# RWKV-7 recurrence and GELU MLP on one core: b' and k' of chunks 4 to 11 turned by VectorE from a second load, and another order of the first chunks

## The chip, the cores and the metric

The kernel runs on one core of a Trainium2 chip. The time of a kernel is the device time of one execution in microseconds (us), given as the median of several runs. TensorE is PE in the profile (PEld is its weight load), VectorE is DVE, ScalarE is ACT, GpSimd is POOL, and SyncE is SP; SPq is SyncE's queue, from which nearly all transfers (DMAs) are issued in order.

## The reference

For each of 4 x 8 pairs of batch and head, a 40 x 40 state is carried over 768 steps; the outputs, joined over the heads to 3072 rows of 320, go through an MLP.

```
for t in range(S):
    y[t]  = r[t] @ state
    Sa    = state @ a[t]
    state = state * w[t] - outer(Sa, b[t]) + outer(v[t], k[t])
x   = y, (B, H, S, D) -> (B*S, H*D)
out = gelu_exact(x @ w_in) @ w_out          # 320 -> 2048 -> 320
```

All inputs but the two MLP weights are float32. The weights come as 64-bit floats, which the kernel turns into float32 itself.

## The kernel before

**Chunks.** The 768 steps are cut into 12 chunks of 64 (c = 0 to 11). Inside a chunk the recurrence is written with matrices over the 64 steps. With cumulative decays (`sums`: a product of the logs of w with a triangle, then Exp), b and k are divided by the decay so far (`scale_b`, `scale_k`: `nb` and `ks`, with time on the partitions) and a is multiplied by it (`scale_a`). `make_N` and `make_A` multiply a' with b' and k' over the head dimension; for these products b' and k' must lie with the head dimension on the partitions, that is turned. N's triangular inverse is made on GpSimd, in 31 columns of two instructions each (`start_inverse`, L604 and L606): the 32 x 32 blocks go out to DRAM and come back spread over all partitions (tiles N, Nb), and the result returns the same way (`store_inverse`, `fetch_inverse`: tiles W, inv, Tt). The corner blocks are joined by small products (`corner`, `joined`: J). From these come X, sa, M, and QY, which holds the new state and the outputs (`make_X` to `make_QY`, `outputs`), and a second load of v and r makes RV.

**Turning.** `flip` (L411) turns a tile on TensorE, as eight 128 x 128 products with the identity into PSUM; ACT copies the result to SBUF. b' (`turn_b`, tile nT), k' (`turn_k`, tile kT) and the state (`turn_state`) are turned so in every chunk. a, r and v are turned so in chunks 0 to 2 only (NT = 3). From chunk 3 on `fetch_pairs` (L147) loads them in a layout of pairs of steps, 32 partitions per group, so that DVE's transpose of 32 x 32 blocks (`turn`, L165) makes the turned tile; such a load has 2 x 2 transfers for a and 2 x 2 x 2 for r and v, each row of 72 or 48 floats. The tiles `a_pairs`, `r_pairs` and `v_pairs` exist once each.

**MLP.** Each chunk gives 128 x 2 rows to the MLP. `mlp` (L784) is cut into eight pieces: four `ph` pieces (40 products with w_in each, then a Gelu on ACT) and four `po` pieces (16 products with w_out each; the third and fourth end with a copy `os` on DVE and the store). `fill()` puts the next piece into TensorE's stream wherever it stands in the program; so the MLP fills the time in which the recurrence waits.

**Weights.** `to_float` (L281) turns 64-bit words into float32, with bit operations on DVE, one Relu on ACT and the last two steps on DVE or on POOL. `convert` and `seconds` advance this by pieces: ten of w_in and sixteen of w_out (f = 0 to 15), all within the first chunks. The raw words are loaded into tiles that are free for the moment; a later load into the same place waits until the piece before is converted.

**Order.** Every engine's queue runs in the order of the program text, which is written by hand (`manual_schedule`). Chunks 0 and 1 and the weights stand one by one (L851 to L1013); then comes a loop from c = 2 (L1015), whose body finishes chunk c, prepares chunk c+1 (n) and loads and begins chunk c+2 (n2). In chunk 2's iteration some pieces are put differently (`if c == 2`). PSUM is used through four buffers of two banks (`duo`). The tile tagged nT holds b' turned and later A; `part` holds the decays and later X.

The lines that the steps below touch: `sums` L393, `turn_b` L462, `turn_k` L474, `make_N` L532, `make_A` L561, `start_inverse` L583, `load_next` L821, `to_float` L281, the start L930 to L1013 and the loop L1015 to L1079.

Of the kernel before, what the change touches and what calls it, by code (L numbers as in the profile page):

```python
# [11 lines left out]
UINT32 = mybir.dt.uint32  # L12
# [7 lines left out]
def kernel(  # L20
# [106 lines left out]


    NT = 3
    paired = {n: const.tile([P, G * H, BW], FP32, name=n + "_pairs") for n in ("a", "v", "r")}  # L130
    w_tile = const.tile([P, G * DM + REST], FP32, name="w_tile")

# [148 lines left out]
    def to_float(dst, words, eng):  # L281


        n = words.shape[1] // 2
        lo, hi = (words.rearrange("p (n x) -> p n x", x=2)[:, :, x] for x in range(2))
        power = work.tile([P, LW // 2], UINT32, tag="power", name="power", bufs=2)[:, :n]
        mant = work.tile([P, LW // 2], UINT32, tag="mant", name="mant", bufs=2)[:, :n]
        nc.vector.tensor_scalar(power, hi, 0x7FF00000, None, ALU.bitwise_and)  # L288
        nc.scalar.activation(power, power, ACT.Relu, bias=rebias, scale=8.0)  # L289
        nc.vector.tensor_scalar(mant, hi, 0x000FFFFF, 0x00100000, ALU.bitwise_and, ALU.bitwise_or)  # L290
        if eng is nc.vector:
            yield
        nc.vector.scalar_tensor_tensor(power, hi, 0x80000000, power, ALU.bitwise_and, ALU.bitwise_or)
        mant_f, power_f, lo_f = mant.bitcast(FP32), power.bitcast(FP32), lo.bitcast(FP32)
        if eng is nc.vector:
            eng.scalar_tensor_tensor(mant_f, lo, 2.0 ** -32, mant, ALU.mult, ALU.add)
            eng.scalar_tensor_tensor(dst, mant_f, 2.0 ** -20, power_f, ALU.mult, ALU.mult)  # L297
        else:
            nc.scalar.mul(lo_f, lo, 2.0 ** -52)
            nc.scalar.mul(mant_f, mant, 2.0 ** -20)  # L300
            eng.tensor_tensor(mant_f, mant_f, lo_f, ALU.add)
            eng.tensor_tensor(dst, mant_f, power_f, ALU.mult)
        yield
# [62 lines left out]
            to = second_raw[f] = at[:, slot * DM:(slot + 2) * DM]  # L366
        nc.sync.dma_start(out=to, in_=src[f * P:(f + 1) * P])

    def words(tag, bufs=1):
        return work.tile([P, 2 * DM], UINT32, tag=tag, name="words", bufs=bufs)  # L370

    def second_convert(f, eng):
        if wide_out:
            yield from to_float(w_out_sb[:, f], second_raw.pop(f), eng)
# [18 lines left out]
    def sums(c):  # L393
        logw = raws.pop((c, "w"))
        cum = duo("cum")[:, :, :DM]
        for g in range(G):
            mm(cum[:, g], cum_m, logw[:, g * DM:(g + 1) * DM])

        pt = duo("wT_ps").rearrange("p e (n t) -> p e n t", t=C)
        for n in range(G * NP):  # L400
            for x in range(2):
                for e in range(2):
                    at = (2 * n + x) * D
                    mm(pt[half(x), e, n], logw[half(e), at:at + HP], cum_m[half(e), half(e)])
        rw = (avs_ring if c in (1, 2) else part_ring)()[:, :, :DM]
        nc.scalar.activation(rw, cum, ACT.Exp, scale=-1.0)
        wp = wp_ring()
        nc.scalar.activation(wp[:, :, 1:].rearrange("p (n e) t -> p e n t", e=2), pt, ACT.Exp)
        decays[c] = rw.rearrange("p g (h d) -> p g h d", h=H), wp

    def flip(src, name):  # L411

        pt = duo(name).rearrange("p g (n t) -> p g n t", n=NP)
        for g in range(G):
            for n in range(NP):
                nc.tensor.transpose(pt[:, g, n], src(g, n), ident)  # L416
        return pt

    def by_pair(t):
        return lambda g, i: t[:, g, 2 * i:2 * i + 2].rearrange("p h d -> p (h d)")  # L420

    def side(name, tag, bufs):
        return work.tile([P, G, NP, P], FP32, tag=tag, name=name, bufs=bufs)

    def parts(t):
        return t.rearrange("p g n (e t) -> p g n e t", e=2)

    def turn_a(c):
        if c < NT:
# [32 lines left out]
    def turn_b(c):  # L462
        t = turned_in[c]
        nT = side("nT", "nT", 1)
        nc.scalar.copy(nT, flip(by_pair(t["nb"]), "nT_ps"))
        t["nT"] = parts(nT)

# [5 lines left out]

    def turn_k(c):  # L474
        t = turned_in[c]
        kT = side("kT", "kT", 1)
        nc.scalar.copy(kT, flip(by_pair(t["ks"]), "kT_ps"))  # L477
        t["kT"] = parts(kT)
# [15 lines left out]
    def turn_r(c):  # L494
        rT = side("rT", "rT", 2)
        if c < NT:
            raw = raws.pop((c, "r"))
            nc.scalar.copy(rT, flip(lambda q, m: raw[:, NP * q + m].rearrange("p g d -> p (g d)"), "rT_ps"))
        else:
            turn(rT.rearrange("p q m (e t) -> p (q m e) t", e=2), c, "r")  # L500
        turned_in[c]["rT"] = parts(rT)
# [175 lines left out]
    def make_X(c):  # L677
        t = turned_in[c]
        if state[0] is None:
            t["xs"] = t["avs"]  # L680
            return
        st = state[0][0]
        X = duo("X")[:, :, :G * NP * D].rearrange("p x (g i d) -> p x g i d", g=G, i=NP)
        for g, i, x, e, q, m in units():
            mm(X[half(e ^ x), x, g, i], t["aT"][half(x, D), g, i, e], st[half(x, D), e, i, g, :D])
        xs = t["xs"] = part_ring()
        nc.vector.tensor_tensor(xs[:, :, :DM], X.rearrange("p x g i d -> p x (g i d)"), t["avs"][:, :, :DM], ALU.add)
# [240 lines left out]
    joined(1)  # L928
    turn_state()
    make_X(1)  # L930
    for f in range(2):
        second_load(f, 2 * f)
    first_load(True, 1, spare_raw[:, :LW])

    sums(2)
    turn_v(1)
    turn_r(1)
    make_RV(1)
    first_pieces(range(NK - 1), 1, nc.gpsimd)
    convert(1)  # L940
    scale_b(2)
    turn_a(2)
    scale_a(2)
    make_sa(1)
    make_saT(1)
    turn_b(2)
    convert(1)
    make_N(2)
    fetch(2, "k", k, nc.sync)
    convert(1)  # L950
    fill()
    convert(1, True)
    scale_k(2)
    nc.gpsimd.memset(spare_st.rearrange("p e i g d -> p (e i g) d")[:, :, D:], 0.0)
    for n in "av":
        unused(paired[n], nc.gpsimd)
    run(start_inverse(2, nc.gpsimd))
    for f in range(2, 8):
        second_load(f, 2 * f)
    first_pieces((NK - 1,), 1, nc.vector)  # L960
    fill()
    make_y2(1)
    make_M(1)
    convert(1, True)
    load_VR(2)
    load_r(2)
    second_load(8, 0, spare_raw)
    second_load(9, 2, spare_raw)
    second_load(10, 0, words("b_raw"))
    second_load(11, 0, words("k_raw"))  # L970
    second_load(15, 0, words("rT", 2))

    second_pieces(range(NF), nc.vector)
    seconds(2)
    fill()
    turn_k(2)
    make_QY(1)
    fill()
    seconds(2)
    outputs(1)  # L980
    pieces.append(mlp(1))
    turn_v(2)
# [2 lines left out]
    make_A(2)  # L985
    unused(paired["r"], nc.vector)
    load_w(3)
    seconds(4, (12, 12))
    load_VR(3)
    load_a(3)  # L990
    logs(3)
    make_av(2)
    sums(3)
    seconds(1, (13, 14))
    fill()
    seconds(3)
    fetch(3, "b", b, nc.sync)
    fetch(3, "k", k, nc.sync)
    turn_a(3)
    turn_state()  # L1000
    seconds(2, (14, 14), last=True)
    scale(3)
    scale_a(3)
    turn_b(3)
    fill()
    make_N(3)
    store_inverse(2)
    fetch_inverse(2)
    run(start_inverse(3, nc.gpsimd))
    load_r(3)  # L1010
    load_v(3)
    turn_k(3)
    turn_corner(2)  # L1013

    for c in range(2, NCH):  # L1015
        n, n2 = c + 1, c + 2
        more, more2 = n < NCH, n2 < NCH
        corner(c)
        make_X(c)
        if c == 2:  # L1020

            pieces.reverse()
            seconds(2, last=True)
            turn_r(n)
        fill()
        if more2:
            load_next(n2)
        joined(c)
        fill()
        make_sa(c)  # L1030
        make_saT(c)
        if c == 2:
            pieces.reverse()
            fill()
        fill()
        make_y2(c)
        make_M(c)
        if c == 2:
            fill()
        if more:  # L1040
            turn_v(n)
        if more2:
            load_v(n2)
        fill()
        if more2:
            logs(n2)
        make_QY(c)
        outputs(c)
        pieces.append(mlp(c))
        fill()  # L1050
        if more2:
            load_VR(n2)
            sums(n2)
        if more:
            make_A(n)
            turn_state()
        if more2:
            scale(n2)
            turn_a(n2)
            scale_a(n2)  # L1060
        fill()
        if more:
            store_inverse(n)
            fetch_inverse(n)
            make_av(n)
        if more2:
            turn_b(n2)
        if more:
            make_RV(n)
        if more2:  # L1070
            turn_r(n2)
        fill()
        if more2:
            make_N(n2)
            run(start_inverse(n2, nc.gpsimd))
            turn_k(n2)
        if more:
            turn_corner(n)
        fill()  # L1079
    fill(1000)  # L1080

# [29 lines left out]
```

## Time and profile before

| | |
|---|---|
| median of 3 runs | 778.99 us (777.88 to 782.61) |
| the profiled execution: time, span | 777.88 us, 776.2 us |
| busy: PE, PEld, DVE, ACT, POOL | 697.1, 563.5, 279.4, 218.0, 307.3 us |
| mean granted TensorE clock | 0.942 |
| bytes moved, packets | 67.81 MB, 268360 |
| one iteration of the loop (from c = 3) | 54.7 us |
| J of chunk 2, J of chunk 3 begin at | 189.0, 256.1 us |

The span is the time from the first to the last instruction; the rest of an execution's time lies around it. In a timeline a line gives start, duration, engine, source line, operation, output <- inputs and how many; a bracket gives the idle time ahead of it and what ended it. A name such as `nT_ps<-ident,nb` says which tiles are written and read.

### The profile page before, as it was taken

How to read it: one execution, taken by the hardware profiler on the slowest of the kernel's cores; microseconds unless marked ns; L12 is line 12 of the kernel's file. 1: busy time of each engine (PE TensorE's matmuls, PEld its weight loads, DVE VectorE, ACT ScalarE, POOL GpSimd, SP SyncE). 2: the span in 40 equal slices, each digit the busy share in tenths (PEclk: the TensorE clock that was granted, in tenths of full speed). 3: DMA queues.
4: the chain of work that ended last, by engine and by line, in shares of the span. 5: the costliest groups of instructions: out<-in, count | busy, mean ns of one | idle time of the engine just before them, and what ended most of it. 6: DMA issues, size and time to landing. Idle time of an engine off the chain costs nothing.

```text
span 776.2 us, 30537 instructions
## 1 busy us (share of the span) xinstructions
PE 697.1 (90%) x13792; PEld 563.5 (73%) x13792; DVE 279.4 (36%) x422; ACT 218.0 (28%) x260; POOL 307.3 (40%) x776
## 2 busy tenths in 40 slices
PE   7446888355999999999999999999999999999997
PEld 5346676244787887887877877878878878778684
DVE  3777375871334124143133242242341341321000
ACT  5123563331223332331331332322322313112020
POOL 3383168500831470560751832823814705500000
PEclk9666899667999999999999999999999999999999
DMA  8886765435823724725535536437237241120100
GB/s 116 138 169 133 152 163 138 79 84 88 136 53 68 142 55 76 141 45 99 113 69 106 96 68 121 80 67 136 61 70 136 59 74 39 26 42 3 26 9 17
DMA packets 268360, 67.81 MB, mean 87 GB/s; under 512 B 256616, under 2 KB 261512, under 8 KB 268232
## 3 DMA queue, kind: packets, MB, share of 16 engines
q1 hardware_dynamic: 268032, 65.71, 44.6%
q8 instruction: 108, 1.77, 1.0%
q14 instruction: 20, 0.16, 0.1%
q10 hardware_dynamic: 200, 0.16, 0.1%
HBM read 51.68 MB, written 10.22 MB: 80 GB/s over the span
## 4 chain that ended last, share of the span: by engine, by line
PE 80%; DVE 6%; DMA 4%; SPq 3%; POOL 3%; issue 2%; ACT 2%; DVEq 0%; ACTq 0%; POOLq 0%
PE po L800 27%; PE ph L792 27%; PE QY L100 6%; PE J L100 2%; PE cum L100 2%; PE X L100 2%; PE wT_ps L100 2%; PE nT_ps L416 2%; PE N_ps L100 1%; PE RV_ps L100 1%; PE sap L100 1%; PE tn_ps L416 1%; PE saT_ps L100 1%; POOL st L606 1%; POOL st L604 1%
## 5 line engine op out<-in xcount | busy, mean ns | idle before, releaser
L792 PE MATMUL ph<-xt,w_in_sb 64*128 64x256 f32 x1920 | 222.7, 384 | 3.7 <-DVE w_in_sb L297 3.7
L800 PE MATMUL po<-w_out_sb,gt 128*128 128x320 f32 x768 | 218.6, 439 | 2.3 <-DVE os L804 2.3
L792 PEld LDWEIGHTS ph<-xt,w_in_sb 64*128 64x128 f32 x1920 | 184.6, 189 | 27.2 <-DVE w_in_sb L297 4.1
L800 PEld LDWEIGHTS po<-w_out_sb,gt 128*128 128x128 f32 x768 | 143.6, 192 | 61.5 <-DVE os L804 4.4
L604 POOL TENSOR_TENSOR tmp<-W,Nb 128x126 f32<-128x126 f32 (+22 forms) x310 | 114.0, 368 | 153.8 <-DMA Nb<-N 130.3
L606 POOL TENSOR_TENSOR W<-W,tmp 128x126 f32<-128x126 f32 (+22 forms) x310 | 115.5, 372 | 24.3
L794 ACT ACTIVATE gt<-ph 128x1024 f32<-128x1024 f32 x48 | 49.2, 1024 | 178.0 <-PE ph L792 177.9
L804 DVE COPY os<-po 128x320 f32<-128x320 f32 x24 | 11.8, 491 | 113.3 <-PE po L800 107.8
L444 POOL TENSOR_TENSOR ks<-k_raw,part 128x640 f32<-128x640 f32 x10 | 15.6, 1562 | 66.0 <-DMA k_raw<-in_k_dram 39.2
L510 DVE TENSOR_TENSOR SM<-M_ps,upper 128x1024 f32<-128x1024 f32 x12 | 14.7, 1224 | 64.1 <-PE M_ps L100 64.1
L594 POOL MEMSET W<- 128x512 f32 x10 | 5.3, 529 | 77.4 <-DMA inv<-W 77.3
L749 DVE TENSOR_TENSOR xt<-QY,wpT 128x512 f32<-128x512 f32 x24 | 15.5, 686 | 55.4 <-PE QY L100 55.4
L477 ACT COPY kT<-kT_ps 128x1024 f32<-128x1024 f32 x12 | 12.1, 1012 | 70.2 <-PE kT_ps L416 70.2
L510 DVE TENSOR_TENSOR VR<-RV_ps,upper 128x1024 f32<-128x1024 f32 x12 | 14.7, 1222 | 47.2 <-PE RV_ps L100 47.2
L671 DVE COPY Tt<-J 32x512 f32<-32x512 f32 x12 | 8.3, 689 | 62.7 <-ACT Tt L671 62.7
L510 DVE TENSOR_TENSOR A<-A_ps,upper 128x1024 f32<-128x1024 f32 x12 | 14.7, 1222 | 39.4 <-PE A_ps L100 39.4
L289 ACT ACTIVATE power<-power,rebias 128x320 uint32<-128x320 uint32 (+1 forms) x26 | 15.9, 622 | 33.7 <-DVE power L288 33.6
L794 ACT ACT_TABLE_LOAD x10 | 12.8, 1283 | 42.2 <-PE ph L792 42.1
L100 PE MATMUL av<-VR,A 64*64 64x40 f32 x768 | 15.2, 240 | 10.5 <-DVE A L510 10.5
L100 PE MATMUL cum<-w_tile,cum_m 128*128 128x320 f32 x44 | 16.4, 501 | 9.1 <-ACT w_tile L391 9.1
L100 PEld LDWEIGHTS av<-VR,A 64*64 64x64 f32 x768 | 13.9, 149 | 14.7 <-DVE A L510 10.7
L578 ACT COPY avs<-av 128x640 f32<-128x640 f32 x12 | 8.3, 693 | 54.1 <-PE av L100 54.1
(154 smaller groups left out, 890.1 us busy)
## 6 DMA issues: line engine op xcount, KB each, us to landing
Nb<-N SPq DMA_DIRECT2D x22, 256.0 KB
VR<-in_v_dram SPq DMA_DIRECT2D x24, 160.0 KB
out_dram<-os SPq DMA_DIRECT2D x48, 80.0 KB
w_tile<-in_w_dram SPq DMA_DIRECT2D x22, 160.0 KB
b_raw<-in_b_dram SPq DMA_DIRECT2D x22, 160.0 KB
k_raw<-in_k_dram SPq DMA_DIRECT2D x22, 160.0 KB
w_out_sb<-in_moe_w_out_dram SPq DMA_DIRECT2D x11, 320.0 KB
N<-N SPq DMA_DIRECT2D x48, 64.0 KB
```

The costliest lines, as they stand in the source:

```text
L100: nc.tensor.matmul(o, lhsT, rhs, start=first, stop=True, skip_group_check=True)
L289: nc.scalar.activation(power, power, ACT.Relu, bias=rebias, scale=8.0)
L416: nc.tensor.transpose(pt[:, g, n], src(g, n), ident)
L444: eng.tensor_tensor(ks[:, :, :, :D], raws.pop((c, "k")), rwv, ALU.mult)
L477: nc.scalar.copy(kT, flip(by_pair(t["ks"]), "kT_ps"))
L510: nc.vector.tensor_tensor(to, pt, upper.unsqueeze(1).to_broadcast([P, 2 * G * NP, C]), ALU.mult)
L604: eng.tensor_tensor(t, W[:, :rows, j:j + 1].to_broadcast([P, rows, rest]), Nb[:, j:j + 1, j + 1:].to_broadcast([P, rows, rest]), ALU.mult)
L606: eng.tensor_tensor(W[:, :rows, j + 1:], W[:, :rows, j + 1:], t, ALU.add)
L749: nc.vector.tensor_tensor(xt[:, :NP, g * P:(g + 1) * P].rearrange("p i (e t) -> p i e t", e=2), Y, wp[:, g, :, :, :C], ALU.mult)
L792: nc.tensor.matmul(ph[:, x, s], w_in_sb[half(x), kt, p * P:(p + 1) * P], xt[half(x), kt], start=kt == 0, stop=kt == NK - 1)
L794: nc.scalar.activation(gt[:, 4 * q:4 * q + 4].rearrange("p (x s) t -> p x s t", x=2), ph, ACT.Gelu)
L800: nc.tensor.matmul(po[:, g], gt[:, f, g * P:(g + 1) * P], w_out_sb[:, f], start=f == 0, stop=f == NF - 1)
```

## The change

Two things are changed. First, from chunk NB = 4 on, b' and k' are no longer flipped on TensorE. b and k are loaded a second time in the layout of pairs, into the tiles of a's and r's pairs once these have been read; DVE transposes them into a tile of the tag `conv` (the two work tiles of the weight conversion, made one), and multiplies them there by a second exponential `en` of the turned decays, which ACT makes beside `wpT`. The rows `nb` and `ks` are still made as before, since QY needs them. `en` takes the buffer of kT, and becomes the turned k'; for that, `make_A(n)` moves in front of `sums(n2)`. `turn_a(n2)` moves forward, behind `make_saT(c)`, and `turn_r(n2)` behind `turn_v(n)`.

```diff
+    NB = 4
...
-        power = work.tile([P, LW // 2], UINT32, tag="power", name="power", bufs=2)[:, :n]
-        mant = work.tile([P, LW // 2], UINT32, tag="mant", name="mant", bufs=2)[:, :n]
+        both = work.tile([P, LW], UINT32, tag="conv", name="conv", bufs=2)
+        power, mant = both[:, :n], both[:, LW // 2:LW // 2 + n]
...
         nc.scalar.activation(wp[:, :, 1:].rearrange("p (n e) t -> p e n t", e=2), pt, ACT.Exp)
         decays[c] = rw.rearrange("p g (h d) -> p g h d", h=H), wp
+        if c >= NB:
+            en = turned_in.setdefault(c, {})["en"] = by_batch(side("en", "kT", 1))
+            nc.scalar.activation(en.rearrange("p (e n) t -> p e n t", e=2), pt, ACT.Exp, scale=-1.0)
...
     def turn_b(c):
         t = turned_in[c]
         nT = side("nT", "nT", 1)
+        if c >= NB:
+            bT = by_batch(side("bT", "conv", 2))
+            turn(bT, c, "b_turned")
+            nT = by_batch(nT)
+            nc.vector.scalar_tensor_tensor(nT, bT, -1.0, t["en"], ALU.mult, ALU.mult)
+            t["nT"] = parts_by_batch(nT)
+            return
...
     def turn_k(c):
         t = turned_in[c]
+        if c >= NB:
+            kT = by_batch(side("k_turned", "conv", 2))
+            turn(kT, c, "k_turned")
+            en = t.pop("en")
+            nc.vector.tensor_tensor(en, kT, en, ALU.mult)
+            t["kT"] = parts_by_batch(en)
+            return
...
(in the loop)
         make_sa(c)
         make_saT(c)
+        if more2:
+            turn_a(n2)
+            fetch_pairs(n2, "b_turned", b, nc.sync, False, paired["a"])
...
         if more2:
             load_v(n2)
+            turn_r(n2)
+            fetch_pairs(n2, "k_turned", k, nc.sync, False, paired["r"])
...
+        if more:
+            make_A(n)
         if more2:
             load_VR(n2)
             sums(n2)
         if more:
-            make_A(n)
             turn_state()
```

Second, the order of the start behind `make_X(1)` is written anew. N of chunk 2 stands behind two `ph` pieces of chunk 0's MLP and no longer in front of them. All five pieces of w_in's second half end on POOL (four before). `store_inverse(2)` and `fetch_inverse(2)` stand in front of N of chunk 3, no longer behind it. All pieces of w_out are converted, and all four `po` pieces of chunk 0's MLP put, ahead of the loop (14 pieces and two `po` before), and the special cases of `c == 2` in the loop are gone. The new order, shortened to the steps that matter:

```
make_X(1); turn_v(1); turn_r(1); make_RV(1)
second_load 0, 1; first_load; fetch k(2); second_load 2 to 7
convert; sums(2); convert; make_sa(1); make_saT(1); scale_b(2); turn_a(2); scale_a(2); convert
fill (ph); turn_b(2); fill (ph); make_N(2); convert; make_y2(1); make_M(1); convert
scale_k(2); start_inverse(2); load_VR(2); load_r(2); second_load 8, 9
seconds(3); fill (ph); turn_k(2); fill (ph); seconds(3); make_QY(1); outputs(1)
turn_v(2); turn_r(2); make_RV(2); make_A(2); load_w(3); fetch b(3)
seconds(2), load 10; logs(3); fetch k(3); load_VR(3); load_a(3); seconds(1), load 11
fill (po); seconds(1), load 12; seconds(1), load 13
make_av(2); sums(3); scale(3); turn_a(3); scale_a(3); turn_state()
fill (po); seconds(2), load 14; turn_b(3); store_inverse(2); fetch_inverse(2)
seconds(1), load 15; load_r(3); load_v(3); seconds(2, last)
fill (po); make_N(3); start_inverse(3); turn_k(3); turn_r(3); turn_corner(2); fill (po)
```

## The prediction

> **What bounds the kernel now.** First the page's slices and the chain's shares: TensorE (PE) carries the chain that ended last, and is full from the eleventh slice on, not before.
>
> ```profile
> PE   7446888355999999999999999999999999999997
> ...
> PEclk9666899667999999999999999999999999999999
> DMA  8886765435823724725535536437237241120100
> ...
> PE 80%; DVE 6%; DMA 4%; SPq 3%; POOL 3%; issue 2%; ACT 2%; DVEq 0%; ACTq 0%; POOLq 0%
> ```
>
> Then the table of windows, columns busy time (and instructions) of PE, PEld, DVE, ACT, POOL, then granted clock, DMA share, GB/s: two stretches of the start, two whole loop iterations.
>
> ```profile
> 120.00:160.00 40.00, 26.80 (x502) 21.55 (x499) 25.57 (x56) 15.01 (x21) 23.85 (x58) 0.74 0.44 105
> 160.00:200.00 40.00, 22.86 (x354) 18.29 (x354) 20.49 (x39) 9.10 (x13) 7.57 (x19) 0.74 0.45 84
> ...
> 296.90:351.50 54.60, 54.60 (x1148) 44.36 (x1148) 17.43 (x21) 16.05 (x18) 24.96 (x66) 1.00 0.48 92
> ...
> 406.30:460.90 54.60, 54.60 (x1148) 44.61 (x1148) 17.33 (x21) 16.05 (x18) 25.17 (x66) 1.00 0.48 91
> ```
>
> In the loop nothing but PE's own work counts; at the start PE idles 13.2 and 17.1 us of 40, and its clock falls to 0.74. So there are two sums. PE's timeline shows the loop's two flips, each between neighbours that follow without a gap, and where the start's large gaps end:
>
> ```profile
> 151.81 2.50 PE L100 MATMUL cum<-w_tile,cum_m 128*128 128x320 f32 x4 [9.10 <-ACT w_tile L391]
> ...
> 170.17 1.94 PE L416 MATMUL nT_ps<-ident,nb 128*128 128x128 f32 x8 [7.92 <-DVE nb L438]
> ...
> 189.03 1.08 PE L100 MATMUL J<-L,N 32*32 32x32 f32 x64 [9.22 <-DVE L L641]
> ```
>
> ```profile
> 352.58 1.09 PE L416 MATMUL nT_ps<-ident,nb 128*128 128x128 f32 x8
> ...
> 360.29 1.09 PE L416 MATMUL kT_ps<-ident,ks 128*128 128x128 f32 x8
> ```
>
> Last the timeline of SyncE's queue (SPq), for the transfers that the new ones are put between:
>
> ```profile
> 369.67 2.90 SPq L162 DMA_DIRECT2D a_pairs<-in_a_dram  x4
> ...
> 376.62 5.48 SPq L159 DMA_DIRECT2D r_pairs<-in_r_dram  x8
> 388.26 5.27 SPq L159 DMA_DIRECT2D v_pairs<-in_v_dram  x8
> ...
> 404.42 2.46 SPq L618 DMA_DIRECT2D inv<-W  x2
> ```
>
> **What the Trainium skill says.** "VectorE: DVE Perf Modes", The three transpose paths: VectorE transposes 32x32 blocks only, into SBUF. The trace agrees: b' and k' can take this path only because the pair layout loads make the blocks whole, as a's do (L167, 1.24 us). "TensorE: Matmul & The Clock Gate", Part 1: after an idle window of some 3.4 us the clock halves until PE has been busy as long. Agrees in kind: behind the 9.22 us gap J and X took 2.9 us where the loop takes 1.75, and the ph after them 6.1 for 4.6, so full speed came back only after some 9 us. "DMA: Bandwidth & Descriptors", Issuing engines are not separate DMA queues: the time to initiate a DMA is usually small relative to the DMA. Here it isn't: the rows of pairs (a, r, v) alone take SPq 13.7 of 54.7 us.
>
> **The loop, part by part** (iterations c=2 to 9, which prepare chunks 4 to 11). Zero is the start of J (365.6 above).
>
> Removed: nT and kT flips. In the chain of waits av starts 351.57 and takes 1.07, RV starts 353.67; N starts 359.26 and takes 1.09, po starts 361.38: 1.03 each, 2.06 per iteration, 8 x 2.06 = 16.5 us. ACT also loses two copies of 1.01.
>
> Added on ACT: the second exp, like wpT's, 1.03. ACT falls from 16.05 to 15.1 of 52.6. It delays the state's copy by 1 us, which y2 needs over 30 us later: nothing.
>
> Added on DVE: two transposes at 1.24 and two products of 1024 columns. Nearest row aT L459: 1.23 alone, 2.57 at worst, when POOL's ks ran; I take 1.24, bounds 5.0 and 7.7 in all. DVE then has 22.4 of 52.6. The order decides: A's mask ends near 34.4, nb 35.9, aT 37.7, b' transposed 38.9, then the nT product waits for av (nT's buffer is A's): 41.7 to 43.0. N needs it at 47.2, so 4 us of cover. Behind it wait RV's mask and os, needed later still. k' comes after L and ends near 53; A needs it 32 us later, and behind it on DVE stand only os (0.5) and, at 54.6, the sum of X. Cost 0; without cover each us late would be paid eight times.
>
> Moved: aT's transpose behind SM's copy (13.5), where a's load (issued by 7) has landed; A in front of cum, so that the old kT is read before the exp overwrites it. Same work: 0. PSUM loses two users.
>
> Added on SPq: per iteration eight loads of a's shape, 2.90 per four, 5.8 us, and 4096 packets. From page part 3, 44.6% of 776.2 us over 268032 packets is 1.29 ns of the 16 engines per packet, so 5.3 us: DMA share 0.48 to about 0.6. Will SPq still be in time? Its rows of one iteration sum to 40.6; with the 2.1 it waits for the store's landing and 1.7 for N's it needs 44.4, with the new ones 50.2 of 52.6. b's four go after r (16.5 to 19.4), before v may start (its buffer is read at 22.6, so v's wait absorbs them); k's four after v (27.9 to 30.8). This pushes the xt moves, VR, the inverse's store and fetch by 2.9: Tt's last load is issued near 48.2, lands near 50.2, L ends 51, J starts 52.6. In the old loop the same slack was 3.3 us (L ended 362.26, J began 365.6); now about 1.6. POOL: N's block is about 1.8 us later, inverse from 7 to 34.4 (27.4 long), its store at 40.7: covered. Loop sum: -16.5.
>
> **The start.** Up to X(1), 85.2 us, both orders are equal. I walk the new order with old durations, all estimates:
> - All five second-half pieces of w_in now go to POOL (1.29 + 1.33 each). The last ends near 120.1; the third ph, which waited for such a piece until 118.6, starts that much later. N(2), now behind the first gelu's ACT table load, is masked near 111 instead of 104; on SPq the six w_out loads now in front of its store (3.2 us) are out by 105, so they cost nothing. The inverse of chunk 2 runs 125 to 152 instead of 118 to 146. Not needed before 165.
> - DVE converts w_out at 2.1 to 2.4 us a piece. Five are done in front of the outputs of chunk 1 instead of three, in time in which DVE waited 8.9 us for a Relu behind a gelu. A(2)'s mask ends near 141.4 (was 140.7).
> - The first po now stands before av(2) and cum(3), in the old 9.10 gap. It needs pieces 0 to 7: the memset ends 142.3, three more pieces 149.4. po ends 150, av 152, cum 154.5 at the low clock.
> - nb(3) has ten pieces in front of it instead of 14, and the exp of cum(3): it ends near 157.5 instead of 170.0, and the 7.92 gap goes. Second po to 162.4, nT(3) 163.5.
> - The third po needs piece 15. Its load stands on SPq behind piece 14's (which waits until piece 11 is converted, 165.3) and behind the store and fetch of the inverse (2.95 for the landing): issued 173, landed 176, converted 180. So po 3 ends 180.7: a new gap, some 13 us of its wait idle. Then N(3), kT(3), po 4: J(2) near 188.5. N(3)'s store stands behind 16 loads of r and v (8.9 us in the old rows) and goes out near 185; its inverse runs to about 221 and is stored at 229, which covers it. The old 9.22 gap goes, as Tt landed by 173.
>
> J(2) was 189.0, but then two po (9 us) were left and J(3) came at 256.1, 67.0 later. Now none is left: 188.5 + 52.6 + 0.5 = 241.6. The gain to J(3) is 14.5, of which 2.1 is the first iteration's flips: -12.4 for the start. Bounds: each us that piece 15 is early or late moves J(2) by one; 9 us earlier if the load is ready when piece 14 is, 12 us later and the gain is gone.
>
> **Sum.** 776.2 - 16.5 - 12.4 = 747.3 span. The profiled execution took 777.88, 1.7 over its span, and the median of the three runs is 1.1 above that: 750.1, so 750.
>
> **Rivals.**
> (B) Start gains nothing: piece 15 or an unseen wait on SPq takes back the 12.4. For: a 16-step chain estimated from single rows. Against: three gaps of 26.2 us in all are refilled or passed. 762.
> (C) SPq slips: the 1.6 us slack before L is used up, each iteration keeps its old period; 779 - 12.4 = 767. For: 50.2 of 52.6. Against: DMA share was 0.19, 0.03 and 0.00 in the windows where b's loads fall, so they shouldn't stretch.
> (D) Both at once, or the change doesn't act: 779.
> (E) Slower: SPq becomes the bound, at Tt before J. The new period is then SPq's own need. It passes the old 54.7 when the eight loads cost 10.3 us instead of 5.8; to lose the start's gain and 1% besides it must reach 54.7 + (12.4 + 7.8)/8 = 57.2, that is 1.6 us a load. The slowest single a_pairs issue took 1.93, so it isn't excluded; the median is 0.49. Then 787 or more.
>
> **Chances.** A (both gains) 0.57, B 0.14, C 0.14, D 0.08, E 0.07. What a measurement can tell from no change is about 1% (7.8 us): faster 0.85, same 0.08, slower 0.07. A alone spans 743 to 757; 742 to 770 takes in B and C and leaves out 0.15 to 0.2. DVE's worst case (7.7) stays within its cover and widens nothing.
>
> **What would show it.** Right: loop windows of about 52.6 with PE full, L ending over 1 us before J, a wait for w_out's piece 15 ahead of J(2) near 188, J(3) near 242. Wrong: PE waiting for L (C, E), for nT before N (DVE's cover was gone), or J(3) near 254 (B).

## The result, and the profile after

The changed kernel took 755.58 us (median of 4 runs, 753.1 to 758.52), the kernel before 780.13 in the same series (777.88 to 782.61): a ratio of 0.9686, 95% interval 0.9634 to 0.9738. The profiled execution is the longest of the four, 758.52 us with a span of 756.8 us, so 19.4 us less than the span of before; between the medians the gain is 24.6 us. Some executions run over 1.5% longer than the fastest of their kernel; the medians and ranges below leave those out. J(3) stands for J of chunk 3, X(1) for X of chunk 1. Line numbers behind the edited functions are shifted: `flip` is L418, the `po` product L823, the products of b' and k' L478 and L496.

The page's slices and the chain's shares:

```profile
PE   7456886884999999999999999999999999999997
...
PEclk9655798986999999999999999999999999999999
DMA  9797666095763754755845746648547441110100
...
PE 78%; DVE 5%; POOL 5%; issue 5%; SPq 4%; DMA 3%; ACT 1%; POOLq 0%; DVEq 0%; ACTq 0%
```

TensorE is still the bound, full from the eleventh slice on as before, though a slice is now 18.9 us and was 19.4. The table of windows (columns as before the change: PE, PEld, DVE, ACT, POOL, then clock, DMA share, GB/s), for the two stretches of the start and one iteration of the loop:

```profile
120.00:160.00 40.00, 29.61 (x454) 22.45 (x455) 32.70 (x63) 14.07 (x21) 33.70 (x74) 0.81 0.57 97
160.00:200.00 40.00, 29.07 (x351) 19.73 (x351) 19.09 (x39) 10.35 (x14) 3.70 (x8) 0.76 0.58 122
```

```profile
302.28:355.33 53.05, 53.05 (x1134) 42.68 (x1133) 22.69 (x25) 14.84 (x17) 25.78 (x66) 1.00 0.60 112
```

The period fell from 54.69 to 53.05 us and PE waits for nothing in it; VectorE went from 17.4 to 22.7 us, ScalarE from 16.05 to 14.84, the DMA share from 0.48 to 0.60. At the start PE idles 10.4 and 10.9 us of 40 instead of 13.2 and 17.1. TensorE's timeline shows where the gaps now are:

```profile
123.96 4.66 PE L815 MATMUL ph<-xt,w_in_sb 64*128 64x256 f32 x24 [3.13 <-POOL w_in_sb L304]
...
184.69 2.77 PE L823 MATMUL po<-w_out_sb,gt 128*128 128x320 f32 x4 [7.09 <-DVE w_out_sb L299]
...
196.18 0.75 PE L100 MATMUL J<-L,N 32*32 32x32 f32 x64
...
249.22 0.75 PE L100 MATMUL J<-L,N 32*32 32x32 f32 x64
```

The gaps of 9.10, 7.92 and 9.22 us ahead of cum, nT's flip and J are gone. A new one stands ahead of the third `po`: 7.09 us for the last piece of w_out, behind three shorter ones for the pieces before it. The first `po` waits for its pieces too, 0.97, 1.97 and 1.78 us. J of chunk 3 begins at 249.22 instead of 256.01.

So the 19.4 us divide thus: J(3) comes 6.8 earlier, of which 1.64 is put down to the first iteration's shorter period; the seven periods from J(3) to J(10) take 371.4 us instead of 383.6 (12.3 less: 54.80 on average before, since two of them had been longer, and 53.05 now); the last stretch is 0.4 shorter.

### The profile page after: what moved, and what is told of

Its sections match the earlier page's. It is cut to its first block, busy times and chain, and to the rows that moved or that the text cites. A ratio compares the mean times of both kernels' runs of the same rounds, so it can differ in the third digit from the quotient of the medians.

```text
span 756.8 us, 30335 instructions
## 1 busy us (share of the span) xinstructions
PE 690.4 (91%) x13664; PEld 550.9 (73%) x13664; DVE 320.8 (42%) x452; ACT 209.1 (28%) x254; POOL 317.6 (42%) x778
## 4 chain that ended last, share of the span: by engine, by line
PE 78%; DVE 5%; POOL 5%; issue 5%; SPq 4%; DMA 3%; ACT 1%; POOLq 0%; DVEq 0%; ACTq 0%
PE po L823 27%; PE ph L815 26%; PE QY L100 5%; PE J L100 2%; PE sap L100 2%; PE cum L100 2%; PE saT_ps L100 2%; PE N_ps L100 2%; PE M_ps L100 2%; DVE W L629 2%; PE av L100 2%; DVE tmp L627 1%; POOL tmp L627 1%; POOL W L629 1%; PE X L100 1%
## 5 line engine op out<-in xcount | busy, mean ns | idle before, releaser
L823 PE MATMUL po<-w_out_sb,gt 128*128 128x320 f32 x768 | 224.5, 445 | 17.4 <-DVE w_out_sb L299 15.5
L823 PEld LDWEIGHTS po<-w_out_sb,gt 128*128 128x128 f32 x768 | 143.9, 193 | 80.5 <-DVE w_out_sb L299 21.0
L629 POOL TENSOR_TENSOR W<-W,tmp 128x126 f32<-128x126 f32 (+22 forms) x310 | 118.2, 381 | 24.3
L453 POOL TENSOR_TENSOR ks<-k_raw,part 128x640 f32<-128x640 f32 x10 | 21.2, 2123 | 34.6 <-DMA k_raw<-in_k_dram 17.5
L678 ACT COPY Js<-J 128x256 f32<-128x256 f32 x12 | 4.5, 372 | 107.7 <-PE J L100 107.7
L291 ACT ACTIVATE conv<-conv,rebias 128x320 uint32<-128x320 uint32 (+1 forms) x26 | 16.0, 622 | 46.4 <-DVE conv L290 46.4
L721 DVE COPY SM<-sap 128x640 f32<-128x640 f32 x12 | 9.9, 824 | 30.3 <-PE sap L100 30.1
L533 DVE TENSOR_TENSOR N<-N_ps,upper 128x1024 f32<-128x1024 f32 x12 | 14.7, 1225 | 18.5 <-PE N_ps L100 18.5
L100 PEld LDWEIGHTS QY<-SM,nb 64*64 64x64 f32 x768 | 18.7, 140 | 5.2 <-issue 3.6
L100 PE MATMUL QY<-SM,nb 64*64 64x104 f32 x768 | 21.3, 263 | 1.3 <-DVE SM L533 1.3
```

The lines of the kernel that those rows point to most:

```text
L100: nc.tensor.matmul(o, lhsT, rhs, start=first, stop=True, skip_group_check=True)
L453: eng.tensor_tensor(ks[:, :, :, :D], raws.pop((c, "k")), rwv, ALU.mult)
L533: nc.vector.tensor_tensor(to, pt, upper.unsqueeze(1).to_broadcast([P, 2 * G * NP, C]), ALU.mult)
L629: eng.tensor_tensor(W[:, :rows, j + 1:], W[:, :rows, j + 1:], t, ALU.add)
L721: nc.vector.tensor_copy(SM.rearrange("p g q (a x) c -> p x (g q a) c", x=2)[:, :, :, :D], sap.rearrange("p x g q a d -> p x (g q a) d"))
L823: nc.tensor.matmul(po[:, g], gt[:, f, g * P:(g + 1) * P], w_out_sb[:, f], start=f == 0, stop=f == NF - 1)
```

## The experiments

### The loop's part and the start's part alone

First the loop is undone and the new start kept. The reason tested is that the two gains stand by themselves; the rival is that one feeds the other.

```diff
-    NB = 4
+    NB = 12
...
-            fetch_pairs(n2, "b_turned", b, nc.sync, False, paired["a"])
...
-            fetch_pairs(n2, "k_turned", k, nc.sync, False, paired["r"])
```

> The changed kernel with NB = 12: the new start and the new order of the loop stay, but b' and k' are flipped on TensorE in every chunk, and the second loads of b and k are left out. Theory F (the loop's gain is the flips' own TensorE time): the loop's period goes from 53.05 us to about 55.05, since two flips of 1.03 come back in front of and behind 64-row groups, and the time to about 771 us. Rival O (the flips were hidden, the order did it): the period stays within 0.3 of 53.05 and the time within 758.

Measured: 775.35 us (770.16 to 779.23, 15 runs), ratio to before 0.9923 (0.9898 to 0.9947). Its loop, in TensorE's timeline:

```profile
338.82 1.16 PE L100 MATMUL A_ps<-aT,kT 40*64 40x64 f32 x64
339.91 1.34 PE L100 MATMUL cum<-w_tile,cum_m 128*128 128x320 f32 x4
341.19 1.16 PE L100 MATMUL wT_ps<-cum_m,w_tile 64*64 64x64 f32 x64
342.28 1.09 PE L418 MATMUL tn_ps<-ident,st 128*128 128x128 f32 x8
...
348.68 1.09 PE L418 MATMUL nT_ps<-ident,nb 128*128 128x128 f32 x8
...
356.40 1.09 PE L418 MATMUL kT_ps<-ident,ks 128*128 128x128 f32 x8
```

J follows J after 55.04 to 55.6 us, so the rival of the expectation (a period still near 53.05) is out: the loop's gain is the flips'. The time missed the expected 771 by 4 us. The shortest period is the one before plus 0.36: with the flips back the loop is slower than it was, and the only thing of the loop that is left changed on TensorE is that A stands in front of cum. The new start without the flips' removal is worth 0.8%, 5 to 6 us, and this is net of some 2.9 us that the loop's new order costs (8 times 0.36, see below).

Then the reverse: the start of before and its special cases for `c == 2`, with the changed loop.

```diff
-    turn_v(1)
-    turn_r(1)
-    make_RV(1)
...
+    first_pieces((NK - 1,), 1, nc.vector)
...
+        if c == 2:
+            pieces.reverse()
+            seconds(2, last=True)
+            turn_r(n)
...
+        if c == 2:
+            fill()
```

> The start of the kernel before, with its special cases in chunk 2's iteration, in front of the changed loop (b' and k' by VectorE from chunk 4 on). Theory F: the loop's period is 53.05 again, J of chunk 2 stands near 189 and J of chunk 3 near 254, and the time is 780.1 - 8 x 1.64 = 767 us; what is missing to 755.6 is the start's own part, 7 to 12. Rival S (the start's new order gave nothing, its extra pieces only moved): within 3 us of 755.6.

Measured: 765.7 us (759.83 to 769.3, 4 runs), ratio 0.9791 (0.9735 to 0.9846), period 53.05. A wait of 9.30 us for L ahead of J(2) is back. J(3) came at 256.90 and not near 254, so here the first iteration gained only 0.4 us. The loop alone brings 2.1% (1.5 to 2.7) and the start alone 0.8%; together they bring 3.1% in the first series and 2.6% in the last one below. So within these intervals they add up, and no sign is seen that one feeds the other; an interplay of a few us would not be seen.

### The order of A and cum

In the changed loop TensorE runs, without a gap:

```profile
276.86 4.58 PE L823 MATMUL po<-w_out_sb,gt 128*128 128x320 f32 x16
281.36 1.16 PE L100 MATMUL A_ps<-aT,en 40*64 40x64 f32 x64
282.45 1.34 PE L100 MATMUL cum<-w_tile,cum_m 128*128 128x320 f32 x4
283.73 1.16 PE L100 MATMUL wT_ps<-cum_m,w_tile 64*64 64x64 f32 x64
284.82 1.09 PE L418 MATMUL tn_ps<-ident,st 128*128 128x128 f32 x8
285.75 4.47 PE L823 MATMUL po<-w_out_sb,gt 128*128 128x320 f32 x16
```

From the first `po` to the second is 8.89 us. In the kernel before, with cum, wT, A, tn in between, it was 8.53:

```profile
338.57 4.57 PE L800 MATMUL po<-w_out_sb,gt 128*128 128x320 f32 x16
342.98 1.24 PE L100 MATMUL cum<-w_tile,cum_m 128*128 128x320 f32 x4
344.15 1.16 PE L100 MATMUL wT_ps<-cum_m,w_tile 64*64 64x64 f32 x64
345.13 1.11 PE L100 MATMUL A_ps<-aT,kT 40*64 40x64 f32 x64
346.17 1.09 PE L416 MATMUL tn_ps<-ident,st 128*128 128x128 f32 x8
347.10 4.47 PE L800 MATMUL po<-w_out_sb,gt 128*128 128x320 f32 x16
```

The shape field (128\*128, 40\*64, 64\*64) shows the reading: in the old order the two groups of full width, `po` and cum, stood side by side, and so did the two of 64, wT and A; now they alternate. The theory is that each change between the two kinds costs something, and the new order has two changes more. So A goes between cum and wT, where it still reads the old kT ahead of the exp that overwrites it:

```diff
-        if more:
-            make_A(n)
         if more2:
             load_VR(n2)
-            sums(n2)
+            sums(n2, lambda: make_A(n))
...
+        if between:
+            between()
```

> The changed kernel, with A's 64 products put between cum and wT in the loop instead of in front of cum. Theory T (the loop gained 1.64 instead of 2.06 because the new order has two more changes between groups of 128-row and of 64-row products in cum's place): cum goes from 1.27 us back to about 1.08, the period from 53.05 to about 52.7, the time to 753 us. Rival (cum is slower because of what VectorE or the transfers do at that moment): the period stays 53.05.

Measured: 754.45 us (752.72 to 756.67, 6 runs), ratio 0.9662 (0.9631 to 0.9692), period 52.70. Its timeline:

```profile
273.48 4.57 PE L825 MATMUL po<-w_out_sb,gt 128*128 128x320 f32 x16
277.89 1.24 PE L100 MATMUL cum<-w_tile,cum_m 128*128 128x320 f32 x4
279.06 1.16 PE L100 MATMUL A_ps<-aT,en 40*64 40x64 f32 x64
280.05 1.11 PE L100 MATMUL wT_ps<-cum_m,w_tile 64*64 64x64 f32 x64
281.09 1.09 PE L420 MATMUL tn_ps<-ident,st 128*128 128x128 f32 x8
282.02 4.47 PE L825 MATMUL po<-w_out_sb,gt 128*128 128x320 f32 x16
```

8.54 us again. The 0.35 us per iteration are the order's, shown by moving one group of products. That the shapes are what counts in the order has a second sign, in the two flips that went. Both were eight products of full width. The nT flip stood between two narrow groups (av and RV); without it the stretch from av to the next `po` is 1.16 us shorter (3.19 before, 2.03 after). The kT flip stood between N, which is narrow, and `po`, which is not; without it the stretch from N to J is 0.83 shorter (6.43, then 5.60). The first removal took two changes of kind away with it and the second none: 0.33 us for two changes, where the order gave 0.35. Eight times 0.35 is 2.8 us, too little for these runs to tell apart from the changed kernel by the clock alone; the period tells it.

### The last piece of w_out

The start's new gap is explained by two timelines of the changed kernel, SyncE's queue and VectorE:

```profile
171.40 0.33 SPq L369 DMA_DIRECT2D w_out_sb<-in_moe_w_out_dram  x1
171.82 1.28 SPq L641 DMA_DIRECT2D inv<-W  x2
176.07 1.93 SPq L651 DMA_DIRECT2D Tt<-inv  x4
178.04 0.98 SPq L655 DMA_DIRECT2D T<-inv  x2
179.07 0.45 SPq L369 DMA_DIRECT2D spare_raw<-in_moe_w_out_dram  x1
```

```profile
182.74 0.33 DVE L290 TENSOR_SCALAR conv<-spare_raw 128x320 uint32<-128x320 uint32 x1 [6.63 <-DMA spare_raw<-in_moe_w_out_dram]
```

Piece 15's words stand behind piece 14's, which wait for a converted piece, and behind the way of the inverse through DRAM. VectorE has nothing to do for 6.63 us; the last steps of piece 14 stand behind the first of piece 15 on VectorE, so they wait too. If this is the gap, an earlier load into a free tile takes it away:

```diff
+    second_load(15, 0, work.tile([P, 2 * DM], UINT32, tag="rT", name="words", bufs=2))
...
-    seconds(1, (15, 0, spare_raw))
+    seconds(1)
```

> The changed kernel, with the raw words of w_out's piece 15 loaded into a buffer of rT right behind those of pieces 8 and 9, instead of behind the store and fetch of chunk 2's inverse. Theory P (the last gap of the start, 7.1 us before the third po, is that load's place in the queue): the gap goes, TensorE keeps its clock, J of chunk 2 comes 7 to 10 us earlier than 196.2 and the time is about 747 us. Rival (Tt or N of chunk 3 comes last anyway): under 2 us.

Measured: 753.57 us (751.47 to 755.02, 4 runs), ratio 0.9647 (0.961 to 0.9683). The wait ahead of the last four products of the third `po`, in TensorE's timeline:

```profile
179.73 2.76 PE L823 MATMUL po<-w_out_sb,gt 128*128 128x320 f32 x4 [1.33 <-DVE w_out_sb L299]
```

From X(1) to J(2) it took 104.0 us, the changed kernel 112.2: 8.2 less, and 7.09 of wait became 1.33. The scatter between executions is smaller than that: in the seven profiled executions of this document that have the new start and the load in its old place, the stretch took 108.1 to 112.2 us, in the three with the load moved 102.1 to 104.0. Yet the expectation was missed: J(2) came at 191.73 and not 7 to 10 us ahead of 196.2, and the median fell by 2.0 where some 8 was expected. In this profiled execution X(1) began at 87.78, in the other at 83.99, though nothing in front of it differs; whether that explains the medians, one execution of each can't show, and the last series below tries it. It is a lesson on its own: X(1) began at 81.4 to 87.8 in the executions with the new start, so an edit there is measured from a mark that it can't move.

### How much room SyncE's queue has

Cases C and E of the prediction rest on the queue. Four more transfers per iteration, and then twelve, of the same rows of k but only four floats of each, into small tiles:

```diff
             fetch_pairs(n2, "k_turned", k, nc.sync, False, paired["r"])
+            for t in again:
+                for x in range(2):
+                    for z in range(2):
+                        rows = k.rearrange("b (i x) (s y) d -> x s (b i) (y d)", x=2, y=2)[x]
+                        nc.sync.dma_start(out=t[x * HP + z * BL:x * HP + (z + 1) * BL],
+                                          in_=rows[n2 * C // 2:(n2 + 1) * C // 2, :, :4])
```

> The changed kernel with four more transfers per iteration on SyncE's queue, right behind the second load of k: the same rows of k, only four floats of each, into a small tile that nobody reads. Nothing is left out. They should take the queue 2.3 to 2.9 us per iteration, and push the loads of Tt by as much, from an issue that ended at 296.2 to about 299, so that L, which began at 299.05 behind other work of VectorE, begins near 301.5 and ends just at J's start of 302.3. Theory Q (about 3 us of slack between the queue and J, as the timeline of the changed kernel reads): period 53.0 to 53.5, time 755 to 759. Rival (C of the prediction, no slack): every us counts, period about 55.5, time about 775. Rival (the queue has much room): 53.05 and no other start of L than 299.

> The same with twelve more transfers per iteration instead of four (three small tiles). Nothing is left out. They should take the queue 7 to 8.7 us; v's wait (1.7 us) stands ahead of them and can't absorb them, the slack ahead of J (about 3) can. Theory Q: TensorE waits for L ahead of each J, period 53.05 + 7.9 - 3 = about 58 at first sight, and between 56 and 58 once the later J also delays what the queue waits for; time 779 to 795, slower than before the change, as case E of the prediction would have it. Rival (transfers are hidden however many): period 53.05 and 755.

Measured with four: 766.84 us (one run). The first periods are 53.05; then TensorE begins to wait a little for L:

```profile
357.54 0.75 PE L100 MATMUL J<-L,N 32*32 32x32 f32 x64
410.78 0.74 PE L100 MATMUL J<-L,N 32*32 32x32 f32 x64
464.13 0.74 PE L100 MATMUL J<-L,N 32*32 32x32 f32 x64 [0.24 <-DVE L L665]
517.62 0.74 PE L100 MATMUL J<-L,N 32*32 32x32 f32 x64 [0.37 <-DVE L L665]
```

The reason stands in VectorE's timeline:

```profile
409.92 0.71 DVE L665 STREAM_TRANSPOSE L<-Tt 128x512 f32<-128x512 f32 x1 [2.47 <-DMA Tt<-inv]
463.28 0.71 DVE L665 STREAM_TRANSPOSE L<-Tt 128x512 f32<-128x512 f32 x1 [2.60 <-DMA Tt<-inv]
```

L now waits 0.8 to 3.2 us for Tt's landing, where in the changed kernel it followed other work of VectorE without a wait. The four took 2.1 us of the queue in most iterations (3.2 and 3.4 in the last two). The first iterations use up the lead that Tt had (L's wait grows from 1.06 over 1.89 to 2.47 us); then the queue sets the pace, with periods of 53.24, 53.35 and 53.49. So 2.1 us more are 0.2 to 0.4 too many, and the room in each iteration is 1.6 to 1.9 us. The expected time, 755 to 759, was missed. From J(3) on it is 6.1 us over the changed kernel (427.7 to the last J, for 421.6); one period of 55.5, in which X also stood 2.09 us for no reason that the trace shows, holds 2.4 of them. The other part of the distance to 755.6 lies in the start, which doesn't differ: the changed kernel itself took 759.83 in the last series below, on the same chip.

With twelve: 804.38 us (one run), slower than before the change. The lines of J in its timeline:

```profile
309.31 1.08 PE L100 MATMUL J<-L,N 32*32 32x32 f32 x64 [5.71 <-DVE L L665]
368.50 0.76 PE L100 MATMUL J<-L,N 32*32 32x32 f32 x64 [3.18 <-DVE L L665]
483.64 1.08 PE L100 MATMUL J<-L,N 32*32 32x32 f32 x64 [4.64 <-DVE L L665]
```

In the seven iterations from J(3) to J(10) the twelve took 7.0 to 8.6 us, 7.8 on average; the period is 57.4 to 60.8, 59.0 on average (663.2 - 249.9 over 7). The added time less the room that the run before showed gives about the same: 53.05 + 7.8 - 1.7 = 59.15. That is above the expected 56 to 58, and the time, 804, above the expected 795. In five of the seven iterations the granted clock is 0.93 to 0.97, and PE is busy for 54.8 to 56.0 us; in the two others it is 1.00. Since the shortest period (57.38) has 0.97 and one of 59.41 has 1.00, these runs don't show that the clock lengthens the period. So case E's mechanism is real, at the place that the prediction gave it: the queue sets the pace once some 1.7 us are added, and its period would pass the old 54.69 at about 3.3 us more (an estimate: 1.7 of room and the 1.64 that the loop had gained).

### How much cover VectorE's work has

Six more transposes of b' ahead of the product that makes nT:

```diff
             turn(bT, c, "b_turned")
+            raws.update({(c, i): raws[c, "b_turned"] for i in range(6)})
+            for i in range(6):
+                turn(bT, c, i)
```

(The copies of the entry are made ahead of the first transpose, which takes its own out.)

> The changed kernel with six more transposes of b' per iteration, between b's transpose and the product that makes nT: 6 x 1.23 = 7.4 us of VectorE. Nothing is left out. In the changed kernel the product waits 2.38 us for av and ends at 292.65, and N needs it at about 296.2: 5.9 us of cover. Theory K (cover as in the prediction): 1.5 us per iteration are not covered, so period 54.5 (54 to 55.5), TensorE waiting for nT ahead of N, time 767 (763 to 775). Rival (VectorE's added work is never on the path): 53.05 and 755. Rival (no cover, each us counts): period 60, time about 814.

Measured: 779.82 us (one run). The products that wait for nT, in TensorE's timeline:

```profile
359.46 1.16 PE L100 MATMUL N_ps<-aT,nT 40*64 40x64 f32 x64 [1.48 <-DVE nT L481]
360.90 4.58 PE L826 MATMUL po<-w_out_sb,gt 128*128 128x320 f32 x16 [0.28 <-DVE os L830]
```

N waits 1.48 us, as the theory had it. Its two numbers were both a little small: the six took 7.7 us (8.92 for all seven in a row, where one takes 1.23), and the cover in the changed kernel is 6.4 (2.38 of wait for av, and 4.0 from nT's end to N, 292.65 to 296.68), of which 0.14 stay between nT's end and N. Behind it 0.28 us more is paid by the `po` that waits for `os`, which stands behind the late work on VectorE. Most periods are 54.95 (two are 56.7 and 56.9), within the 54 to 55.5 that was expected; the time missed the range of 763 to 775, by those two periods and by a J(2) at 198.6.

### Both improvements, and w_in's last piece

The two edits that helped, together; and besides them the last piece of w_in on VectorE, for the 3.13 us wait of the third `ph`:

```diff
-    first_pieces(range(NK), 1, nc.gpsimd)
+    first_pieces(range(NK - 1), 1, nc.gpsimd)
+    first_pieces((NK - 1,), 1, nc.vector)
```

> The changed kernel with two edits together: A between cum and the turned sums (as e3_A_between), and piece 15 of w_out loaded into a free tile behind pieces 8 and 9 (as e4_piece15_early). Nothing is left out. By the traces the first is worth 0.35 us in each of 8 iterations (2.8), the second about 8 between X of chunk 1 and J of chunk 2; by the medians they were worth 1.1 and 2.0. Theory (the traces are right, the medians hide it behind starts that differ by some us between executions): 745 to 750, X(1) to J(2) 104. Rival (the start gives the 8 us back somewhere ahead of J(2)): 752 to 753.

> As e8_both, and besides the last piece of w_in ends on VectorE instead of GpSimd, as it did before the change. Nothing is left out. In the changed kernel the third ph waits 3.13 us for GpSimd's last piece, which ended near 124. Theory (that wait is on the start's path, as a step of the prediction had it): it goes, J(2) comes up to 3 us nearer to X(1), 742 to 748. Rival (VectorE, which has 2.6 us more to do ahead of the pieces of w_out, is the start's limit): no gain or up to 2.6 us more than e8_both.

> The changed kernel once more, beside the last two on the same chip, as the base of their comparison. Nothing is left out. 755.6 as before if the chip's start doesn't matter; X(1) to J(2) 108 to 112 and a period of 53.05 in any case.

Measured on one chip, against 778.51 for before:

| kernel | median (range), us | ratio to before | X(1) to J(2), us | period, us |
|---|---|---|---|---|
| the changed kernel again | 759.83 (754.39 to 760.09) | 0.9736 (0.9696 to 0.9777) | 111.8 | 53.05 |
| both edits | 749.93 (745.17 to 754.71) | 0.9631 (0.9588 to 0.9675) | 102.1 | 52.70 |
| both, and w_in's piece on VectorE | 747.64 (745.12 to 752.49) | 0.9608 (0.9566 to 0.965) | 102.6 | 52.70 |

Both edits bring 9.9 us against the changed kernel of the same series, and the intervals don't touch: the theory that the trace's 8 and 2.8 us are real holds, with 749.93 at the edge of its 745 to 750. With w_in's piece moved the third `ph` waits as long as ever, for the other engine:

```profile
119.18 5.11 PE L817 MATMUL ph<-xt,w_in_sb 64*128 64x256 f32 x24 [3.02 <-DVE w_in_sb L299]
```

On VectorE that conversion stands behind the mask of M (113.05), which waits for TensorE. The wait is not GpSimd's; it changed its name. The time fell into the theory's range of 742 to 748 all the same, which is luck: the wait that should have gone is still there, X(1) to J(2) is no shorter, and the 2.3 us between the last two medians lie within their intervals.

## Why the prediction was right, and where its sizes were off

**The number.** 750 was predicted within 742 to 770, and 755.6 came. That range held the rivals B (762) and C (767) too, so the number alone would not have told them from A. The prediction's own sign is less kind: J(3) at 249.2 lies nearer to B's 254 than to A's 242. What bears the mechanism out is the loop's windows and the experiments; the start's size is what went wrong.

**The bound.** "In the loop nothing but PE's own work counts" held: 53.05 us busy of 53.05. The flips went and nothing took their place.

**The loop's sum.** Predicted 2.06 per iteration and 16.5 in all. The two flips' removal gave 1.99 (the 1.16 and 0.83 above), and the period with like shapes side by side again confirms it: 54.69 - 52.70. The term that was missed stands under "Moved": "A in front of cum ... Same work: 0" costs 0.36 (8.89 for 8.53), 2.9 in eight iterations; with the flips back the loop is slower by it, with A behind cum faster by it.

**ScalarE, VectorE.** VectorE's four instructions took 1.2 us each, the lower bound, and the order of events was the predicted one: the product waits for av, as in the changed kernel's VectorE timeline.

```profile
287.81 1.23 DVE L169 STREAM_TRANSPOSE bT<-a_pairs 128x1024 f32<-128x1024 f32 x1
291.42 1.23 DVE L478 SCALAR_TENSOR_TENSOR nT<-bT,en 128x1024 f32<-128x1024 f32 x1 [2.38 <-PE av L100]
```

It ends 4.0 us ahead of N, as predicted; with six transposes more the whole cover (2.38 + 4.0) was spent and then paid for. What the prediction left out cost nothing either: the product of aT, which took 1.23 us while GpSimd was idle, now begins while GpSimd's ks still runs and takes 1.83, and ks takes 2.19 for 1.55.

**SyncE's queue.** Predicted 50.2 of 52.6 and a slack of 1.6. The eight loads took 5.0 us in one iteration (2.14 and 2.89, in others 4.0 to 6.3), v's wait, 4.1 to 6.3 us in the kernel before from chunk 3's iteration on, shrank to 0.1 to 3.1, and the run with four transfers more put the room at 1.6 to 1.9. So cases C and E were some 1.7 and 3.3 us per iteration away and not more.

**The clock.** That "full speed came back only after some 9 us" misreads the trace. In windows of 1 us the kernel before shows a granted clock of 0.50 from J at 189.03 on, and 0.98 and more from 195.0 on: 6 us, not 9. The `ph` of 6.1 us that the sentence counts as slow was at full speed in its second half. No term of the sum uses the 9 us.

**The start.** Every step came in the predicted order, with the new gap at piece 15, but 12.4 us were promised and 5.2 came (6.8 less the 1.64 of flips). The terms, from marks in the trace; the predicted ones use X(1) at 83.25 in the kernel before:

| stretch | predicted | changed kernel | other executions |
|---|---|---|---|
| X(1) to the third ph | 36.9 | 40.0 | 37.0 (A between), 39.0 (again) |
| third ph to the end of the third po | 60.6 | 63.5 | 62.1 (A between), 63.4 (again) |
| end of the third po to J(2) | 7.8 | 8.7 | 9.0, 9.5 |
| J(2) to J(3) | 53.1 | 53.0 | 53.7, 53.1 |

The four add 3.1 + 2.9 + 0.9 - 0.1, and X(1) itself came 0.7 later: 7.5 of the 7.6 us by which J(3) (249.2) missed 241.6. The first scatters between executions of the same text: of the eight that end w_in on GpSimd and show the third `ph` cleanly, three took 37.0 to 37.1 and five 39.0 to 40.0, so the predicted 36.9 is the short case and not the usual one; what decides is not settled. In the second a term was mis-sized: "DVE converts w_out at 2.1 to 2.4 us a piece". While GpSimd's inverse ran, a piece took 2.74 (147.46 to 150.20), with the inverse done 1.92 (168.09 to 170.01). The three pieces ahead of the first `po`, for which 7.1 us were allowed, took 8.1; that is 1.0 of the 2.9, and the rest is spread over steps that no run took apart. Two of its instructions, on one kernel's VectorE timeline:

```profile
148.83 0.72 DVE L298 SCALAR_TENSOR_TENSOR conv<-w_out_sb,conv 128x320 f32<-128x320 uint32 x1
...
168.96 0.49 DVE L298 SCALAR_TENSOR_TENSOR conv<-w_out_sb,conv 128x320 f32<-128x320 uint32 x1
```

The old kernel's conversions, from which 2.1 to 2.4 was taken, straddled the end of its inverse: five of the sixteen were finished under it, in the new order eight. That GpSimd is the cause is read from the coincidence (here, and in the loop's aT and ks); it wasn't tried apart.

**The rivals.** B (the start gains nothing) is refuted by the first two experiments, though the start gained less than half of what was forecast. C: the slack wasn't used up. E: excluded here. The queue becomes the bound some 1.7 us per iteration further on, and with 7.8 us more the kernel was slower than before the change.

**The sum.** 747.3 of span was predicted, 756.8 measured in the execution at hand, 9.5 more: 7.2 at the start, and 2.2 in the loop (0.42 in each of 8 iterations, 3.4, less 0.8 that two long iterations of before had cost and 0.4 at the end). The median, 755.6, is nearer to its 750 (5.6) only because the profiled execution was the longest of the four. Of the estimates along the start's chain nearly all were on the hopeful side, so their errors added up.

## What to carry to other kernels

When one engine is full, take work from it and check three slacks in the timeline of the others: the cover ahead of each consumer, the queue that issues the new transfers, and the order of neighbours on the full engine itself, where a move of "the same work" isn't free (0.36 us here). At the start of a kernel, where everything waits for something, read the last gap ahead of the loop and ask which single load could have been issued earlier: here one moved load took 8.2 us out of the stretch to J(2) in the trace, where the whole rewritten start had gained 5.2. Measure such an edit from a mark ahead of it to a mark behind it, since executions of the same text differ by several us there.

## What the runs showed of the hardware

Products of different tile shapes, alternating (128\*128, 40\*64, 128\*128, 64\*64), cost 0.36 us more than the same products with like shapes side by side, some 0.17 for each change. That it is the shapes, and not another difference between these groups, is supported by the two flips but not tried apart. VectorE's two-input instructions on 128 x 320 took 0.72 us under GpSimd's load and 0.49 without; in the loop aT's product took 1.83 us beside GpSimd's ks and 1.23 alone. The DMA share rose by 0.12 for 4096 packets more per iteration, as the packet price of the old page had given, and no product in the loop waits for it. After a gap of 9.2 us TensorE's clock was granted at half for 6 us of work. And TensorE stood up to 3.2 us "for issue", in which the trace shows no reason, in the first 120 us of every execution, at different instructions (saT, M, J, and others), and in four of them later too. Whether this is why the medians of one kernel moved from 755.6 to 759.8 between two series isn't settled.
